# The diagonal of eight attention steps on TensorE, with values and state as separate factors

## The chip, the cores and the metric

The kernel runs on one core of a Trainium2 chip. The metric is the time of one execution on the device in microseconds, the median of several runs. A profiled execution has a time of its own, and a span from its first to its last instruction, on which every row of the trace is placed.

## What is computed

A linear attention with decay over 768 tokens (4 batches, 8 heads, head dimension 48), and behind it two dense two-layer blocks over the 3072 resulting tokens of width 384, inner width 2048. Weights arrive in double precision.

```python
for t in range(S):
    cur = np.einsum('bhd,bhe->bhde', u[None] * kt, vt)
    y[:, :, t] = np.einsum('bhd,bhde->bhe', rt, state + cur)
    state = wt[:, :, :, None] * state + np.einsum('bhd,bhe->bhde', kt, vt)
...
h = x @ w_in                    # block 1
g = np.where(h >= 1, h, np.where(h <= -1, 0.0, (h + 1) ** 2 / 4))
x = g @ w_out
...
h = x @ w_in                    # block 2
g = np.where(h > 0.0, h, np.exp(np.minimum(h, 0.0)) - 1.0)
out = g @ w_out
```

## The kernel before

**Attention.** The tokens are cut into chunks of 64; a step takes one chunk of all heads of two batches, so there are 24 steps of 128 tokens, each with the work of 16 heads in two halves of the 128 partitions (`hh`) and eight columns of tiles (`u`). Steps 0 to 3 make the first block of 512 tokens (`BLOCKS[0]`), and write it straight into the input tile `x_hl` of the dense block (`out_x`, `x_act`); the later ones go through the DRAM tensor `xd` (`out`, `out_act`). `QuotientAttention.stages` gives a step's seven stages: `decays` (two scans over the decays, L444 and L447, and one product in place that scales k and r, both in the tile `rk_sb`, L448), `operands` (a transpose of k on TensorE, copies of r into `tt` by `r_act`, L316 and L317, and the diagonal term: from k and r in token-major form, `tok_sb`, two products L458 and L460, a sum L462, and a spread of the sums onto the diagonal of `a_sb`, L464), `scores` (16 products of k and r on TensorE, L471; decay of the state, L356), `masked` (the state is copied into the free halves of the value tile `vs_sb`, L336 and L337; the scores under the mask are written into `a_sb`, L485), `placed` (`a_sb` is copied into the free halves of `tt`, L488 and L489; update of the state, L366 and L372), `out` (one product per tile: values stacked on the state, times scores stacked on r, L343 or L424) and `stored`. The stacking is what the four copies into `tt` and the two into `vs_sb` are for: 64 partitions hold values and scores, the other 64 state and r.

**Dense blocks.** Six parts of 512 tokens, each through two blocks, make 12 jobs (`ji`) of 16 slots (`f`). A slot multiplies into `h` (9 matmuls, L175), applies the activation (`act1` or `act2`, on ScalarE alone or on ScalarE and VectorE by `ON_ACT`), splits the result into a high and a low part (L220, L221) and multiplies into `y` (9 matmuls, L230). The weights of a slot are converted from double precision first (`weight_stages`, L121 to L139, five instructions on VectorE and three on ScalarE).

**Order.** Nothing loops at run time: everything is put into a plan by tick and rank (`at`), sorted, and emitted in that order; the framework then orders each engine's instructions by it and by what is ready in its own model. Step s begins at its tick in `START` (0, 4, 9, 12) or `AT1`, `AT2`, `AT`, relative to `t0` = 29 or to a job; its stages take one tick each with the ranks `RANK_A`. Weights of slot f begin at `WSTART[f]`, and the first slot runs at tick 29. So steps 0 to 7 lie ahead of the slots or beside the first two of them. `TOK_POOL` names the diagonal instructions that GpSimd takes instead of VectorE, `WARM` the numbers of matmuls on zeros that are issued in the first four steps' stages (L154), with no result that is used.

**Buffers.** `rk_sb` and `w_sb` have two buffers each, so step s+2 is loaded when step s no longer reads; `tok_sb` and `a_sb` have one, `vs_sb` and `tt` two. In PSUM `h` has two, the attention's transpose, scores and updates share two.

## Time and profile before

| | |
|---|---|
| runs, us | 942.51, 942.46, 940.45; median 942.46 |
| profiled execution, us | 942.46 |
| its span, us | 940.6 |
| TensorE busy (weight loads) | 97% (78%) |
| VectorE, ScalarE, GpSimd busy | 67%, 62%, 3% |
| mean granted TensorE clock | 0.98 of 2.4 GHz |

Shares over the whole span hide that the span has stages with different limits. It is read by stretches: for each, which engine is full, and whether TensorE, which is nearly always shown as busy, also loads weights at the rate that it has where nothing else is near its limit.

### The profile page before, as it was taken

How to read it: one execution, taken by the hardware profiler on the slowest of the kernel's cores; microseconds unless marked ns; L12 is line 12 of the kernel's file. 1: busy time of each engine (PE TensorE's matmuls, PEld its weight loads, DVE VectorE, ACT ScalarE, POOL GpSimd, SP SyncE). 2: the span in 40 equal slices, each digit the busy share in tenths (PEclk: the TensorE clock that was granted, in tenths of full speed). 3: DMA queues.
4: the chain of work that ended last, by engine and by line, in shares of the span. 5: the costliest groups of instructions: out<-in, count | busy, mean ns of one | idle time of the engine just before them, and what ended most of it. 6: DMA issues, size and time to landing. Idle time of an engine off the chain costs nothing. (4 is left out here: it accounts for less than half of the span.)

```text
span 940.6 us, 15005 instructions
## 1 busy us (share of the span) xinstructions
PE 911.7 (97%) x5985; PEld 736.7 (78%) x5985; DVE 634.1 (67%) x929; ACT 584.6 (62%) x944; POOL 29.0 (3%) x41
## 2 busy tenths in 40 slices
PE   9767999999999999999999999999999999999996
PEld 4555778788888888888888888888888888888885
DVE  8999999976566667643499995554554555555452
ACT  5778999886688877877799963433433423423332
POOL 1001001000010000000000000000000000000000
PEclk9958999999999999999999999999999999999998
DMA  7866644452234324321554400100200201000001
GB/s 222 272 213 212 234 151 145 140 166 60 93 94 127 110 87 125 111 84 25 178 200 135 167 35 1 49 20 1 67 1 1 68 1 32 35 1 1 34 1 37
DMA packets 42014, 87.81 MB, mean 93 GB/s; under 512 B 5072, under 2 KB 18512, under 8 KB 41936
## 3 DMA queue, kind: packets, MB, share of 16 engines
q1 hardware_dynamic: 41936, 86.77, 28.6%
q8 instruction: 49, 0.80, 0.4%
q14 instruction: 29, 0.24, 0.1%
HBM read 72.59 MB, written 14.16 MB: 92 GB/s over the span
## 5 line engine op out<-in xcount | busy, mean ns | idle before, releaser
L230 PE MATMUL y<-g_hl,w_hl 128*128 128x512 f32 x1728 | 429.7, 392 | 0.0
L175 PE MATMUL h<-x_hl,w_hl 128*128 128x512 f32 x1728 | 427.2, 391 | 1.7 <-ACT w_hl L138 0.8
L175 PEld LDWEIGHTS h<-x_hl,w_hl 128*128 128x128 f32 x1728 | 323.7, 188 | 71.1 <-DVE e_g L195 2.1
L230 PEld LDWEIGHTS y<-g_hl,w_hl 128*128 128x128 f32 x1728 | 321.1, 188 | 67.9 <-ACT g_hl L220 0.3
L221 DVE TENSOR_TENSOR g_hl<-e_g,g_hl 128x512 fp32r<-128x512 f32 x192 | 134.3, 700 | 102.4 <-ACT g_hl L220 102.0
L220 ACT CAST g_hl<-e_g 128x512 fp32r<-128x512 f32 x192 | 119.6, 623 | 101.7 <-DVE e_g L213 77.7
L210 ACT ACTIVATE e_g<-e_g 128x512 f32<-128x512 f32 x92 | 58.1, 632 | 153.1 <-DVE e_g L209 153.1
L213 DVE SCALAR_TENSOR_TENSOR e_g<-e_g,h 128x512 f32<-128x512 f32 x96 | 66.0, 687 | 60.8 <-ACT e_g L210 57.0
L209 DVE TENSOR_SCALAR e_g<-h 128x512 f32<-128x512 f32 x92 | 63.6, 691 | 44.0 <-PE h L175 43.4
L195 DVE TENSOR_TENSOR e_g<-h,e_g 128x512 f32<-128x512 f32 x96 | 65.7, 685 | 38.5 <-ACT e_g L188 38.3
L186 ACT ACTIVATE e_g<-h,half 128x512 f32<-128x512 f32 x87 | 60.2, 692 | 35.1 <-PE h L175 34.7
L187 ACT ACTIVATE e_g<-e_g,one 128x512 f32<-128x512 f32 x87 | 63.6, 731 | 1.5
L188 ACT ACTIVATE e_g<-e_g 128x512 f32<-128x512 f32 x87 | 55.6, 639 | 1.0
L366 PEld LDWEIGHTS ds<-vk_sb,rk_sb 64*64 64x64 f32 x704 | 20.8, 138 | 20.6 <-DVE st L372 7.7
L366 PE MATMUL ds<-vk_sb,rk_sb 64*64 64x48 f32 x704 | 24.4, 226 | 10.7 <-DVE st L372 6.6
L448 DVE TENSOR_TENSOR rk_sb<-rk_sb,w_sb 128x1024 f32<-128x1024 f32 x24 | 30.0, 1252 | 4.7 <-DMA rk_sb<-in_rkq 4.5
L471 PEld LDWEIGHTS sc<-tt,rk_sb 64*64 64x64 f32 x768 | 27.7, 144 | 6.9 <-issue 4.0
L139 DVE TENSOR_TENSOR w_hl<-w_z,w_hl 128x768 fp32r<-128x768 f32 x32 | 30.6, 958 | 3.1 <-ACT w_hl L138 3.0
L471 PE MATMUL sc<-tt,rk_sb 64*64 64x64 f32 x768 | 32.2, 233 | 0.2 <-ACT tt L488 0.2
L133 DVE CUSTOM_DVE_ANT_0 w_z<-w_raw,w_z 128x1536 uint16<-128x1536 uint16 x32 | 31.3, 977 | 0.5 <-ACT w_raw L122 0.2
L444 DVE TENSOR_TENSOR_SCAN w_sb<-w_sb,start 128x520 f32<-128x520 f32 x24 | 29.6, 1234 | 2.5 <-DMA w_sb<-in_wq 2.4
L464 POOL TENSOR_TENSOR a_sb<-eyef,z_sb 128x512 f32<-128x512 f32 x17 | 21.3, 1254 | 324.7 <-DMA xd<-a_sb 138.4
(65 smaller groups left out, 613.8 us busy)
## 6 DMA issues: line engine op xcount, KB each, us to landing
w_raw<-in_w SPq DMA_DIRECT2D x32, 768.0 KB, 4.7
rk_sb<-in_rkq SPq DMA_DIRECT2D x24, 512.0 KB, 3.9
tok_sb<-in_tokq SPq DMA_DIRECT2D x24, 384.0 KB, 3.3
w_sb<-in_wq SPq DMA_DIRECT2D x24, 260.5 KB, 3.9
x2d<-y_o SPq DMA_DIRECT2D x21, 256.0 KB, 2.0
x_hl<-x2d SPq DMA_DIRECT2D x6, 768.0 KB, 4.4
out_y<-y_o SPq DMA_DIRECT2D x18, 256.0 KB, 2.0
vk_sb<-in_vkq SPq DMA_DIRECT2D x22, 192.0 KB, 4.0
```

The source lines that it names most:

```text
L175: self.nc.tensor.matmul(h[:, :n], w[:, a, k * P:(k + 1) * P], x[:, b, k, :n], start=i == 0, stop=i == 8)
L186: nc.scalar.activation(out=g, in_=h[:, :n], func=AF.Relu, bias=self.half, scale=-0.5)
L187: nc.scalar.activation(out=g, in_=g, func=AF.Relu, bias=self.one, scale=-1.0)
L188: nc.scalar.activation(out=g, in_=g, func=AF.Square)
L195: nc.vector.tensor_tensor(out=g, in0=h[:, :n], in1=g, op=ALU.max)
L209: nc.vector.tensor_scalar_min(g, h[:, :n], 0.0)
L210: nc.scalar.activation(out=g, in_=g, func=AF.Exp)
L213: nc.vector.scalar_tensor_tensor(out=g, in0=g, scalar=1.0, in1=h[:, :n], op0=ALU.subtract, op1=ALU.max)
L220: nc.scalar.copy(gh[:, 0, :n], g)
L221: nc.vector.tensor_tensor(out=gh[:, 1, :n], in0=g, in1=gh[:, 0, :n].bitcast(F32), op=ALU.subtract)
L230: self.nc.tensor.matmul(y[d][:, :n], w[:, a, DM + d * P:DM + (d + 1) * P], g[:, b, :n], start=first and j == 0, stop=last and j == 2)
L471: nc.tensor.matmul(ps[64 * hh:64 * hh + 64, u], c["rk"][q:q + 64, 0, NU - 1 - u], c["tt"][q:q + 64, hh, u], start=True, stop=True)
```

## The change

For the steps below `DIAG` = 8:

- The diagonal term no longer comes from `tok_sb`. `diagonal`, at the head of `decays`, scales k by u per partition (four ScalarE instructions of 128x128 into `tt`), multiplies it with r on TensorE (16 products into a PSUM tile that shares the two buffers of `h`), and `operands` multiplies the result by the identity into `tt` (one VectorE instruction). The token loads, the two products, the sum and the spread are left out. A tile `u_col` with u along the partitions is loaded once by two DMAs.
- Values and state aren't stacked. The scores stay where they are masked (`c["a"]` is half of `tt`), r is read from `rk_sb`, the state is copied to a tile of zeros (`sz`), and `out` or `out_x` multiply twice into the same PSUM: values times scores, and state times r (the first step of a sequence once). The four copies into `tt` are left out. The halves of `vs_sb` that hold no values are set to zero on GpSimd.

The GpSimd share changes (`TOK_POOL`: the spread of steps 12 and later stays on GpSimd, that of steps 8 to 11 is on VectorE), one slot of job 0, two of job 1 go from ScalarE alone to both engines and job 6 has one more on ScalarE (`ON_ACT`), 24 matmuls on zeros fewer are issued, and ticks and ranks of the plan are others.

```diff
--- before.py
+++ after.py
@@ -31,26 +31,27 @@
 
 
 START = [0, 4, 9, 12]
-AT1 = [-13, -10, -7, -3]
-AT2 = [8, 13, 17, 20]
+AT1 = [-14, -11, -8, -4]
+AT2 = [7, 13, 17, 20]
 AT = [-6, 0, 3, 6]
 T0 = 11
-WSTART = [21, 22, 20, 25, 24, 29, 33, 37, 37, 39, 37, 42, 44, 44, 46, 46]
+WSTART = [21, 22, 21, 25, 27, 29, 33, 34, 37, 36, 37, 42, 43, 43, 45, 45]
 W2, W2_STEP = 4, 1.65
 X_POOL = [0, 1, 1] + [ji % 2 ^ 1 for ji in range(3, 12)]
 W_AHEAD, X_AHEAD, X_SPLIT = 1, 2, 1
 
-RANK_W = [[148, 62, -48], [103, 102, -10]]
-RANK_A = [[80, 146, 173, 72, 35, 21, 85], [39, 103, 199, 65, -3, 0, -18]]
-RANK_S = [[-38, 51, 56, -11, -26], [-4, 37, 46, 56, -7]]
-
-ON_ACT = {0: 27501, 5: 28415, 6: 34836}
-TOK_POOL = {(6, 1), (7, 1), (7, 2), (6, 0)} | {(s, 2) for s in range(8, NSTEP)}
+RANK_W = [[148, 66, -48], [97, 102, -10]]
+RANK_A = [[80, 109, 173, 72, 35, 21, 56], [25, 103, 199, 36, -3, 0, 53]]
+RANK_S = [[-38, 51, 71, -11, -26], [-4, 37, 46, 94, -7]]
+
+ON_ACT = {0: 27493, 1: 49119, 5: 28415, 6: 9268}
+DIAG = 8
+TOK_POOL = {(s, 2) for s in range(12, NSTEP)}
 RAW = {f: NF // 2 + f for f in range(NF // 2)} | {10: 14, 11: 15}
 SPLIT = 7
 NMORE = 5
 
-WARM = [[3, 3, 3, 3, 3, 3, 3], [1, 2, 0, 3, 2, 2, 2], [2, 1, 4, 3, 4, 1, 2], [3, 2, 2, 1, 2, 3, 2]]
+WARM = [[3, 3, 3, 3, 3, 3, 3], [1, 1, 0, 1, 1, 1, 1], [1, 1, 1, 1, 1, 1, 1], [1, 1, 1, 1, 1, 1, 1]]
 LIMIT = 2.0 ** 64
 
 
@@ -293,6 +294,10 @@
 
         return u
 
+    def apart(self, s):
+
+        return False
+
     def load_consts(self):
         self.nc.sync.dma_start(self.u_sb, self.io["ur"])
         self.nc.sync.dma_start(self.idt, self.io["ident"])
@@ -306,6 +311,9 @@
         s, nc = c["s"], self.nc
         t = self.a1.tile([P, 2, NU * CH], F32, name="vs_sb", bufs=2)
         c["vs"] = vs = t[:, :, :NU * vx.shape[-1]].rearrange("p h (u d) -> p h u d", u=NU)
+        if self.apart(s):
+            nc.gpsimd.memset(t[64:128, 0], 0.0)
+            nc.gpsimd.memset(t[0:64, 1], 0.0)
         nc.sync.dma_start(vs[0:64, 0], vx[s, 0])
         nc.sync.dma_start(vs[64:128, 1], vx[s, 1])
         if not c["last"]:
@@ -332,9 +340,9 @@
         self.nc.scalar.copy(c["kT"], c["ktp"])
 
     def state_act(self, c):
-        st = self.st
-        self.nc.scalar.copy(c["vs"][64:128, 0, :, :D], st[64:128].rearrange("p a b d -> p (a b) d"))
-        self.nc.scalar.copy(c["vs"][0:64, 1, :, -D:], st[0:64].rearrange("p a b d -> p (a b) d"))
+        st, to = self.st, c.get("sz", c["vs"])
+        self.nc.scalar.copy(to[64:128, 0, :, :D], st[64:128].rearrange("p a b d -> p (a b) d"))
+        self.nc.scalar.copy(to[0:64, 1, :, -D:], st[0:64].rearrange("p a b d -> p (a b) d"))
 
     def out(self, c):
         av, nc = self.av, self.nc
@@ -380,6 +388,7 @@
     def __init__(self, tc, ctx, io, xd):
         super().__init__(tc, ctx, io, xd, 2, 2)
         nc, c = self.nc, self.const
+        self.zs = {}
         self.eye = c.tile([P, 2, CH], I32, name="eye")
         self.eyef = c.tile([P, CH], F32, name="eyef")
         self.start = [c.tile([P, NU, CE], F32, name=f"start{i}") for i in range(2)]
@@ -391,6 +400,9 @@
     def vu(self, u):
         return NU - 1 - u
 
+    def apart(self, s):
+        return s < DIAG
+
     def kT_tile(self, c):
         return c["rk"][:, 0].rearrange("p (a b) c -> p a (b c)", b=2)
 
@@ -401,6 +413,10 @@
         super().load_consts()
         self.nc.sync.dma_start(self.eye, self.io["eyeq"])
         self.nc.sync.dma_start(self.eyef, self.io["eyefq"])
+        self.u_col = self.const.tile([P, 4, 1], F32, name="u_col")
+        self.nc.gpsimd.memset(self.u_col, 0.0)
+        for o, row in ((0, 64), (64, 0)):
+            self.nc.sync.dma_start(self.u_col[o:o + D], self.io["ur"][row:row + 1].rearrange("o p d -> d p o"))
 
     def load(self, s):
         c, nc, io = self.new(s), self.nc, self.io
@@ -409,20 +425,46 @@
         c["rk"] = self.a2.tile([P, 2, NU, CH], F32, name="rk_sb")
         nc.sync.dma_start(c["rk"], io["rkq"][s])
 
+    def sz(self, s):
+
+        n = CH if s < BLOCKS[0] else D
+        if n not in self.zs:
+            z = self.a1.tile([P, 2, NU, D], F32, name="tok_sb") if n == D else self.place()
+            self.nc.gpsimd.memset(z, 0.0)
+            self.zs[n] = z
+        return self.zs[n]
+
     def load_tok(self, c):
         c["tok"] = self.a1.tile([P, 2, NU, D], F32, name="tok_sb")
         self.nc.sync.dma_start(c["tok"], self.io["tokq"][c["s"]])
 
+    def factors(self, c, hh, u):
+
+        if c["s"] >= DIAG:
+            return [(c["vs"][:, hh, self.vu(u)], c["tt"][:, hh, u])]
+        return [(c["vs"][:, hh, self.vu(u)], c["a"][:, u])] + [(c["sz"][:, hh, self.vu(u)], c["rk"][:, 1, u])] * (not c["first"])
+
+    def out(self, c):
+        av, nc = self.av, self.nc
+        for u in range(NU):
+            for hh in range(2):
+                h = self.factors(c, hh, u)
+                for i, (v, t) in enumerate(h):
+                    nc.tensor.matmul(av[64 * hh:64 * hh + D, u], v, t, start=i == 0, stop=i == len(h) - 1)
+
     def out_x(self, c):
 
         nc = self.nc
         av = c["av"] = self.av.rearrange("p u c -> p (u c)")[:, :3 * TS].rearrange("p (k b t) -> p k b t", k=3, b=2)
         for b in range(2):
             for k, parts in ((0, ((0, 0),)), (1, ((1, 32),)), (2, ((0, 32), (1, 0)))):
-                for i, (hh, o) in enumerate(parts):
+                n = len(self.factors(c, 0, 0))
+                for i in range(n * len(parts)):
+                    hh, o = parts[i // n]
                     for p in range(4):
-                        nc.tensor.matmul(av[32 * p:32 * p + 32, k, b], c["vs"][:, hh, self.vu(2 * p + b), o:o + 32],
-                                         c["tt"][:, hh, 2 * p + b], start=i == 0, stop=i == len(parts) - 1)
+                        v, t = self.factors(c, hh, 2 * p + b)[i % n]
+                        nc.tensor.matmul(av[32 * p:32 * p + 32, k, b], v[:, o:o + 32], t,
+                                         start=i == 0, stop=i == n * len(parts) - 1)
 
     def x_act(self, c, x, t):
 
@@ -439,7 +481,21 @@
         def flat(t):
             return t.rearrange("p u c -> p (u c)")
 
+        def diagonal():
+            ku = c["tt"][:, 1]
+            for p in range(4):
+                j = NU - 2 - 2 * p
+                nc.scalar.activation(out=ku[:, j:j + 2], in_=c["rk"][:, 0, j:j + 2], func=AF.Copy, scale=self.u_col[:, p])
+            c["z"] = z = self.ph.tile([P, NU * CH], F32, name="z", tag="h").rearrange("p (u c) -> p u c", u=NU)
+            for u in range(NU):
+                for hh in range(2):
+                    q = 64 - 64 * hh
+                    nc.tensor.matmul(z[64 * hh:64 * hh + 64, u], ku[q:q + 64, NU - 1 - u], c["rk"][q:q + 64, 1, u],
+                                     start=True, stop=True)
+
         def decays():
+            if s < DIAG:
+                diagonal()
             back, w = c["w"][:, :NU * CE], c["w"][:, NU * CE:2 * NU * CE]
             nc.vector.tensor_tensor_scan(out=back, data0=free_ap(c["w"], 0, P, 2 * NU * CE, [[-1, NU * CE]]),
                                          data1=flat(self.start[0]), initial=0.0, op0=ALU.mult, op1=ALU.add)
@@ -450,9 +506,14 @@
         def operands():
             if not c["last"]:
                 self.k_transpose(c, c["rk"][:, 0])
-            self.r_act(c, c["rk"][:, 1])
+            if s >= DIAG:
+                self.r_act(c, c["rk"][:, 1])
             w = free_ap(c["w"], 0, P, 0, [[CE, 2 * NU], [1, CH]])
             nc.scalar.activation(out=w, in_=w, func=AF.Square, accum_out=self.sums[:, s:s + 1])
+            a = c["a"] = c["tt"][:, 0] if s < DIAG else self.a1.tile([P, NU, CH], F32, name="a_sb")
+            if s < DIAG:
+                nc.vector.tensor_mul(a, free_ap(self.eyef, 0, P, 0, [[0, NU], [1, CH]]), c["z"])
+                return
             tok = c["tok"]
             e = [nc.gpsimd if (s, i) in TOK_POOL else nc.vector for i in range(3)]
             e[0].tensor_mul(tok[:, 0].rearrange("p (a b) d -> p a b d", b=2), tok[:, 0].rearrange("p (a b) d -> p a b d", b=2),
@@ -460,7 +521,6 @@
             e[1].tensor_mul(tok[:, 0], tok[:, 0], tok[:, 1])
             z = self.a1.tile([P, NU], F32, name="z_sb")
             nc.vector.tensor_reduce(out=z, in_=tok[:, 0], op=ALU.add, axis=AX.X)
-            a = c["a"] = self.a1.tile([P, NU, CH], F32, name="a_sb")
             e[2].tensor_mul(a, free_ap(self.eyef, 0, P, 0, [[0, NU], [1, CH]]), free_ap(z, 0, P, 0, [[1, NU], [0, CH]]))
 
         def scores():
@@ -468,8 +528,8 @@
             for u in range(NU):
                 for hh in range(2):
                     q = 64 - 64 * hh
-                    nc.tensor.matmul(ps[64 * hh:64 * hh + 64, u], c["rk"][q:q + 64, 0, NU - 1 - u], c["tt"][q:q + 64, hh, u],
-                                     start=True, stop=True)
+                    nc.tensor.matmul(ps[64 * hh:64 * hh + 64, u], c["rk"][q:q + 64, 0, NU - 1 - u],
+                                     (c["rk"][:, 1] if s < DIAG else c["tt"][:, hh])[q:q + 64, u], start=True, stop=True)
             if not c["last"]:
                 self.k_act(c)
             if c["first"]:
@@ -478,15 +538,16 @@
                 self.decay_state(free_ap(c["w"], 0, P, CH, [[CE, NU], [0, D]]))
 
         def masked():
-            self.state_act(c)
-            if x is not None:
-                nc.gpsimd.memset(c["vs"][64:128, 0, :, D:], 0.0)
-                nc.gpsimd.memset(c["vs"][0:64, 1, :, :16], 0.0)
+            if s < DIAG:
+                c["sz"] = self.sz(s)
+            if not (c["first"] and s < DIAG):
+                self.state_act(c)
             nc.vector.copy_predicated(c["a"], free_ap(self.eye, 0, P, 0, [[0, NU], [1, CH]]), c["sc"])
 
         def placed():
-            nc.scalar.copy(c["tt"][0:64, 0], c["a"][0:64])
-            nc.scalar.copy(c["tt"][64:128, 1], c["a"][64:128])
+            if s >= DIAG:
+                nc.scalar.copy(c["tt"][0:64, 0], c["a"][0:64])
+                nc.scalar.copy(c["tt"][64:128, 1], c["a"][64:128])
             if not c["last"]:
                 self.state_pe(c)
                 self.state_add(c)
@@ -677,6 +738,8 @@
         moe = Moe(tc, mctx)
         actx = ExitStack()
         att = QuotientAttention(tc, actx, io, xd)
+        att.ph = moe.ph
+        att.place = lambda: moe.place(NF - 1)[0].tile([P, 2, NU, CH], F32, name="state_z", tag="w")
         moe.staging(actx, 2, 3)
         plan = {}
 
@@ -719,7 +782,8 @@
                 at(0, 0, lambda: ys.update({0: [moe.py[0].tile([P, 512], F32, name=f"y{d}") for d in range(3)]}))
                 at(0, 1, lambda: moe.warm(ys[0][0], 6))
             at(tick - 4 if tick >= 4 else 0, 0 if tick < 4 else 85, load)
-            at(max(tick - 1, 0), 86, lambda: att.load_tok(att.ctx[s]))
+            if s >= DIAG:
+                at(tick - 1, 86, lambda: att.load_tok(att.ctx[s]))
             at(tick + 1, 87, lambda: att.load_v(att.ctx[s], io["vxp" if s < BLOCKS[0] else "vxq"], io["vkq"]))
             for i, rank in enumerate(RANK_A[int(s >= BLOCKS[0])]):
                 at(tick + i, rank, lambda i=i: st["s"][i]())
```

## Rows read from the trace of the kernel before

**Rows 1.** Table of windows: stretch, length, busy us (instructions) by engine, clock, DMA share, GB/s.
```profile
25.00:40.00 15.00, 12.94 (x340) 8.95 (x339) 14.33 (x26) 10.45 (x19) 0.40 (x2) 1.00 0.83 259
40.00:64.00 24.00, 13.02 (x174) 10.83 (x171) 22.93 (x34) 16.91 (x28) 2.19 (x2) 0.58 0.69 235
64.00:85.00 21.00, 15.77 (x185) 12.16 (x184) 18.31 (x30) 15.49 (x24) 1.60 (x1) 0.75 0.70 235
95.00:130.00 35.00, 34.63 (x204) 27.57 (x204) 35.00 (x52) 34.12 (x56) 1.64 (x1) 1.00 0.62 205
130.00:170.00 40.00, 40.00 (x316) 32.31 (x314) 39.81 (x62) 39.38 (x65) 3.07 (x1) 1.00 0.47 150
200.00:300.00 100.00, 100.00 (x826) 81.40 (x826) 63.62 (x96) 74.46 (x123) 5.78 (x5) 1.00 0.35 108
```

**Rows 2.** Timeline, VectorE, 32 to 37 us: start, us, instruction, idle before it.
```profile
32.66 0.56 DVE L458 TENSOR_TENSOR tok_sb<-tok_sb,u_sb 128x384 f32<-128x384 f32 x1 [0.67 <-DMA tok_sb<-in_tokq]
...
34.07 1.23 DVE L444 TENSOR_TENSOR_SCAN w_sb<-w_sb,start 128x520 f32<-128x520 f32 x1
35.23 0.53 DVE L462 TENSOR_REDUCE z_sb<-tok_sb 128x8 f32<-128x384 f32 x1
35.67 0.20 DVE L446 RECIPROCAL start<-w_sb 128x8 f32<-128x8 f32 x1
35.85 0.69 DVE L464 TENSOR_TENSOR a_sb<-eyef,z_sb 128x512 f32<-128x512 f32 x1
36.46 0.55 DVE L432 TENSOR_TENSOR x_hl<-av,x_hl 128x384 fp32r<-128x384 f32 x1
```

**Rows 3.** Timeline, VectorE where GpSimd works too, steps 6 and 7.
```profile
58.13 2.01 DVE L448 TENSOR_TENSOR rk_sb<-rk_sb,w_sb 128x1024 f32<-128x1024 f32 x1
...
82.98 0.55 DVE L462 TENSOR_REDUCE z_sb<-tok_sb 128x8 f32<-128x384 f32 x1 [0.90 <-POOL tok_sb L460]
...
90.84 1.80 DVE L133 CUSTOM_DVE_ANT_0 w_z<-w_raw,w_z 128x1536 uint16<-128x1536 uint16 x1
```

**Rows 4.** Groups by form, whole span: count, busy us, mean ns, idle before.
```profile
L195 DVE TENSOR_TENSOR e_g<-h,e_g 128x512 f32<-128x512 f32 x96 | 65.7, 685 | 38.5 <-ACT e_g L188 38.3
L133 DVE CUSTOM_DVE_ANT_0 w_z<-w_raw,w_z 128x1536 uint16<-128x1536 uint16 x32 | 31.3, 977 | 0.5 <-ACT w_raw L122 0.2
L448 DVE TENSOR_TENSOR rk_sb<-rk_sb,w_sb 128x1024 f32<-128x1024 f32 x24 | 30.0, 1252 | 4.7 <-DMA rk_sb<-in_rkq 4.5
L349 ACT COPY a_sb<-av 128x512 f32<-128x512 f32 x20 | 11.4, 572 | 1.2 <-issue 1.2
L190 ACT ACTIVATE e_g<-h,half 128x512 f32<-128x512 f32 x9 | 6.4, 710 | 1.9 <-PE h L175 1.9
L431 ACT CAST x_hl<-av 128x384 fp32r<-128x384 f32 x4 | 1.9, 464 | 0.0
L388 POOL MEMSET start<- 128x520 f32 x2 | 1.0, 534 | 0.0
```

**Rows 5.** Timeline, TensorE: scores at either clock, matmuls on zeros.
```profile
18.43 1.15 PE L471 MATMUL sc<-tt,rk_sb 64*64 64x64 f32 x32
...
34.25 1.48 PE L154 MATMUL y<-zero 128*128 128x512 bf16 x6
...
41.52 2.19 PE L471 MATMUL sc<-tt,rk_sb 64*64 64x64 f32 x32
```

**Rows 6.** Timeline: L448 of steps 0 and 2, and the reload of rk.
```profile
6.38 1.23 DVE L448 TENSOR_TENSOR rk_sb<-rk_sb,w_sb 128x1024 f32<-128x1024 f32 x1
...
16.53 0.33 SPq L410 DMA_DIRECT2D rk_sb<-in_rkq  x1
...
20.61 1.21 DVE L448 TENSOR_TENSOR rk_sb<-rk_sb,w_sb 128x1024 f32<-128x1024 f32 x1
```

**Rows 7.** Timeline: a GpSimd memset with a VectorE product beside it.
```profile
18.63 0.20 POOL L484 MEMSET vs_sb<- 64x128 f32 x1
18.65 0.53 DVE L458 TENSOR_TENSOR tok_sb<-tok_sb,u_sb 128x384 f32<-128x384 f32 x1
```

## The prediction

> **What bounds the kernel now.** I read three views in this order. First the table of windows [rows 1]: busy time of each engine in stretches of the span. The reader is to see three regimes. From 25 to 85 us VectorE (DVE) is busy 14.33 + 22.93 + 18.31 = 55.6 of 60 us (93%), TensorE (PE) only 12.94 + 13.02 + 15.77 = 41.7 of 60, and its granted clock falls to 0.58 and 0.75 in the mean, so part of even that work ran at the lower level, 1.2 GHz. From 95 us on PE is full, and from 130 to 170 us PE, DVE and ScalarE (ACT) are all full. From 200 us on DVE is down to 64%, PE stays at 100%. Whether PE is at its own rate from 130 to 170, or only looks busy while it waits for DVE, is read from the weight loads: their share is 32.31/40 = 81%, as in 200:300 (81.40/100), where DVE cannot be the limit. So from about 100 us PE does its remaining list at full rate, and an edit pays only if it lets this regime begin earlier: what comes before is a start-up set by DVE. It holds the eight attention steps that the change touches and the first weight conversions.
>
> Second, the DVE timeline inside the start-up [rows 2]: the instructions stand shoulder to shoulder, each begins about 0.08 us before the one ahead of it has ended, so a removed instruction is worth the distance between starts, not its duration. Third, the places where DVE and GpSimd (POOL) run side by side [rows 3], and the typical durations [rows 4].
>
> The profiled execution took 942.46 us, which is also the median of the runs, for a span of 940.6: the sum below is made on the span, and the same 1.9 us lie around it afterwards.
>
> **DVE, what goes.** In each of steps 0 to 7 the diagonal's token-major work goes: two products, a sum and a spread onto the diagonal. By distance between starts the product is taken at 0.48 (its duration 0.56 less the overlap), the sum 35.67 - 35.23 = 0.44, the spread 36.46 - 35.85 = 0.61 [rows 2]: 2 x 0.48 + 0.44 + 0.61 = 2.01. One instruction comes in its place: identity times the scores that PE left in PSUM, the same 128x512, taken at the 0.61 of the spread, since DVE's product L195 of the same shape with an operand from PSUM lasts 685 ns [rows 4], as long as the spread's 0.69 [rows 2]. Net 1.40 per step, for steps 0 to 5 8.4. Step 6 has its two products on POOL: there the sum and the spread (1.05) go, the new product (0.61) comes, and the 128x1024 product beside POOL took 2.01 instead of 1.25 [rows 3, 4], 0.76 more. That is 1.2. Step 7 has one product on DVE (0.48), an idle 0.90 in front of the sum while POOL finishes, the sum (0.44), and a weight instruction that took 1.80 beside POOL's spread against 0.98 [rows 3, 4], less 0.61: 2.0. The idle 0.67 for the landing of the token tile [rows 2] goes with its load. Together 8.4 + 1.2 + 2.0 + 0.7 = 12.3 us of a DVE-bound stretch.
>
> The Trainium skill, "SBUF — State Buffer", section on the doors into SBUF, says that VectorE and GpSimd share a port pair that is locked for a whole instruction, so that the other one "fully blocks". The two stretched rows agree in kind. By that rule alone step 6 would give back POOL's whole two products rather than 0.76, about 1.4 us more in the sum. The same rule speaks against the change's new POOL memsets, 16 of 64x512, against DVE instructions in a two-port mode. The rows show a memset beside a DVE product with two inputs that took its ordinary 0.53 [rows 7], and none beside the other kind: memsets are charged nothing; if each of the eight in steps 4 to 7 blocked DVE for its length (0.53 at 128x520 [rows 4]), that would be 4.2 us.
>
> **DVE, what comes back.** (a) The start. The first 128x1024 product of rk began at 6.38 us [rows 6], as soon as its operands were there. Now a column of u must land first (two more DMAs of single elements in the queue of SP, issued behind the constants and in front of step 1's loads, at 0.33 us an issue or more [rows 6]), then ACT scales k (1.2, below) and PE does 32 diagonal passes (1.15 [rows 5]). If the column lands with rk, that is 2.35 us later than 6.38; the scans of step 1 can fill a part. Bounds 0.5 and 4 us, taken at 2.0. (b) In every step the product L448 overwrites rk in place, so it must now wait for the diagonal, which reads rk before it. ACT's part: four 128x128 with a scale from memory; from 710 ns at 512 columns and (572 - 464)/128 = 0.84 ns a column [rows 4], 710 - 384 x 0.84 = 387 ns each, some 1.2 us overlapped. PE's part: 1.15 at full clock, 2.19 at the lower one, as the scores' 32 [rows 5]. Chain about 2.5 to 3.7 us with hand-overs; the two scans and the reciprocal in front of L448 cover about 2.4 (35.23 - 34.07 = 1.16 for a scan, twice, and a little for the reciprocal [rows 2]). Behind a stalled L448 everything on DVE waits, weight conversion too. Bounds 0 and 2.3 us a step; taken at 0.3 for seven steps, 2.0, since a step's operands usually lie there long before its scans. (c) Behind 95 us DVE gets four spreads back from POOL (steps 8 to 11) and three activations move partly from ACT (one slot of job 0, two of job 1): 7 x 0.6 = 4.2 us in a stretch where DVE is 99% busy [rows 1]; fewer stretched instructions and the emptier DVE from 170 on take most of it. Bounds 0 and 4.2, taken at 1.0.
>
> Sum: 12.3 - 2.0 - 2.0 - 1.0 = 7.3 us.
>
> **The other engines.** ACT loses four copies of 512 columns a step (some 0.57 each, by the 128x512 one [rows 4]) and gains 4 x 0.39: 0.7 us less a step. It was less busy than DVE from 25 to 85 [rows 1], so I count this at nothing; the way from the masked scores to the output gets two copies, 1.1 us, shorter. The eight token loads of 384 KB leave SP's queue and the DMA engines (share 0.83 from 25 to 40 us [rows 1]): a cover, not a term. PE gains 32 passes of diagonal a step (1.15), a second set of passes for the output of steps 1 to 7 (taken as the scores' too, 1.15) and loses 24 warm-up matmuls (1.48/6 = 0.25 each, 6 us, mostly ahead of 25 us) [rows 5]. Of that some 6 x 1.15 + 7 x 1.15 = 15.0 us, less about ten warm-ups, 2.4, fall between 25 and 85, 12.6 us into an idle of 18.3. This leaves 5.7 us by which the stretch can shrink before PE binds, if the clock stays as it was; were it at 2.4 GHz throughout, 13.02 x 0.42 + 15.77 x 0.25 = 9.4 us more. So PE allows a gain between 5.7 and 15.1, and the 7.3 lies inside it, near the lower end.
>
> **Who holds rk.** Before, rk's buffer is free after the state update: its reload for step 2 was issued at 16.53, and L448 of step 2 began at 20.61 [rows 6], practically at the landing. Now the output reads r straight out of rk, so the reload comes after the output, by 1.15 us and a hand-over or more later, and the diagonal stands between landing and L448. In steps 2 to 4 this chain (reload 4.1, diagonal 2.5, product 1.25, scores 1.15, then mask, state and an output of 2.3: some 12 to 13 us for two steps) is about as long as two steps of DVE's own work. I count on it being hidden there, since outputs come earlier as well.
>
> **Rivals.** (1) The gain is eaten in the start: the rk chain holds steps 1 to 5 at their old distance, so that their 5 x 1.4 = 7 us are idle time instead, or PE binds at the low clock. Then 0 to 2 us are left: about 941. For it: L448 of step 2 had no slack; against: DVE was 96% busy from 25 to 40 us, so it seldom stood waiting for a reload there. (2) Slower: the diagonal is not hidden behind the scans. With PE at the lower clock and ACT one pair of copies behind, the chain is 3.7 + 1.0, less 2.4 of cover, so L448 stalls 2.3 us in each of eight steps, 18.4, against 12.3 - 3.0 of net savings: 9 us slower, about 951. It decides from (12.3 - 3.0)/8 = 1.2 us of stall per step. For it: the clock is low from 40 to 64 us, and fewer warm-ups remain. Against: the loads are issued steps ahead, so the diagonal can run before DVE comes to the scans. (3) Better: no stall, and the fuller PE keeps its clock: 12 to 15 us, 928 to 930.
>
> **How the numbers follow.** Forecast 942.46 - 7.3 = 935. Chances: forecast with its bounds (930 to 939.5) 0.58, rival 3 0.12, rival 1 0.16, rival 2 0.14. About 0.3% (2.8 us) is what a measurement of this kernel can tell from no change: faster 0.70, same 0.16, slower 0.14. The range leaves out rival 2's far part and the tip of rival 3: 926 to 945.
>
> **What would show it.** Right: the groups L458, L460 and L462 count 16 instead of 24 each; DVE busy from 10 us to the point where the share of weight loads reaches 80% is shorter by some 9 us; that point lies some 7 us earlier; the stretch behind it is of unchanged length. Wrong: idle time in front of L448 released by PE or ACT above 1.2 us a step (rival 2); reloads of rk later than before with DVE idle behind them, or PE busy over 95% already from 40 us (rival 1). The prediction as a whole would fail if the regime behind 100 us was not PE's: then the moved DVE work would show there as new PE gaps.

## The result, and the profile after

The changed kernel took 933.04 us (median of four runs, 931.84 to 936.03), the kernel before 942.42 (four runs, 940.45 to 942.51): a ratio of 0.991, 95% interval 0.989 to 0.9925. That is 9.4 us less. Forecast were 935.0, in a range of 926 to 945. The profiled execution of the changed kernel took 931.84 for a span of 930.0, against 942.46 and 940.6 before, so 10.6 us have to be found in the two traces.

First the table of windows of the changed kernel, in the stretches and columns of [rows 1] (busy time of TensorE, of its weight loads, of VectorE, ScalarE and GpSimd; then clock, DMA share, GB/s):

```profile
25.00:40.00 15.00, 10.46 (x325) 8.72 (x316) 15.00 (x24) 11.13 (x22) 2.08 (x4) 1.00 0.77 252
40.00:64.00 24.00, 19.63 (x540) 17.46 (x540) 23.49 (x37) 19.29 (x39) 3.12 (x6) 0.93 0.70 228
64.00:85.00 21.00, 19.15 (x307) 15.82 (x304) 20.62 (x33) 17.10 (x31) 0.00 (x0) 1.00 0.70 208
95.00:130.00 35.00, 34.93 (x235) 27.83 (x234) 34.77 (x53) 33.93 (x57) 0.00 (x0) 1.00 0.37 119
130.00:170.00 40.00, 40.00 (x300) 32.32 (x298) 39.79 (x61) 35.15 (x59) 0.00 (x0) 1.00 0.40 127
200.00:300.00 100.00, 100.00 (x842) 81.00 (x842) 64.14 (x98) 74.29 (x121) 4.29 (x4) 1.00 0.35 105
```

From 25 to 85 us VectorE (DVE) is busy 15.00 + 23.49 + 20.62 = 59.1 of 60 us, before 55.6 [rows 1]: the start-up is still DVE's, more so than before. TensorE (PE) does 49.2 us of work there instead of 41.7, and its granted clock is 0.93 and 1.00 where it was 0.58 and 0.75. From 130 us on the rate of the weight loads has not changed: they take 32.32 of 40 us, before 32.31 [rows 1]. So the gain lies ahead of that. How much lies there can be counted. These are the matmuls of the dense blocks, called expert matmuls below (the lines L175 and L230, one row each) in the window up to 100 us of the kernel before: busy us and count on PE, then clock, DMA share, GB/s:

```profile
0.00:100.00 100.00, 14.59 (x49) 0.85 0.71 231
0.00:100.00 100.00, 4.85 (x18) 0.85 0.71 231
```

And of the changed kernel (L176 and L231):

```profile
0.00:100.00 100.00, 16.19 (x64) 0.98 0.75 238
0.00:100.00 100.00, 10.85 (x45) 0.98 0.75 238
```

That is 67 before and 109 after, 42 more. What one is worth shows late in the changed kernel, in a window where PE does nothing else:

```profile
800.00:900.00 100.00, 100.00 (x443) 82.84 (x442) 51.10 (x74) 31.73 (x52) 0.00 (x0) 1.00 0.02 9
```

443 in 100 us are 0.226 us each, and 42 x 0.226 = 9.5 us: nine tenths of the 10.6 are won by 100 us. (Both traces hold all 3456 expert matmuls, 12 jobs of 16 slots with 18 each, so the counts lack none.)

What DVE did to get there is read from its groups up to 100 us. Before:

```profile
L448 DVE TENSOR_TENSOR rk_sb<-rk_sb,w_sb 128x1024 f32<-128x1024 f32 x8 | 10.5, 1316 | 0.1
L133 DVE CUSTOM_DVE_ANT_0 w_z<-w_raw,w_z 128x1536 uint16<-128x1536 uint16 x7 | 7.5, 1070 | 0.0
L139 DVE TENSOR_TENSOR w_hl<-w_z,w_hl 128x768 fp32r<-128x768 f32 x6 | 5.7, 949 | 2.4 <-ACT w_hl L138 2.4
L464 DVE TENSOR_TENSOR a_sb<-eyef,z_sb 128x512 f32<-128x512 f32 x7 | 4.8, 684 | 0.0
L462 DVE TENSOR_REDUCE z_sb<-tok_sb 128x8 f32<-128x384 f32 x8 | 4.3, 541 | 0.9 <-POOL tok_sb L460 0.9
L458 DVE TENSOR_TENSOR tok_sb<-tok_sb,u_sb 128x384 f32<-128x384 f32 x7 | 3.9, 552 | 0.9 <-DMA tok_sb<-in_tokq 0.9
L460 DVE TENSOR_TENSOR tok_sb<-tok_sb 128x384 f32<-128x384 f32 x6 | 3.3, 552 | 0.1
```

After (the lines have moved: L448 is now L504, L133 is L134, L139 is L140, and L515 is the new product):

```profile
L504 DVE TENSOR_TENSOR rk_sb<-rk_sb,w_sb 128x1024 f32<-128x1024 f32 x9 | 10.9, 1215 | 0.5 <-PE z L493 0.4
L134 DVE CUSTOM_DVE_ANT_0 w_z<-w_raw,w_z 128x1536 uint16<-128x1536 uint16 x8 | 7.6, 951 | 0.0
L140 DVE TENSOR_TENSOR w_hl<-w_z,w_hl 128x768 fp32r<-128x768 f32 x8 | 7.6, 956 | 0.0
L515 DVE TENSOR_TENSOR tt<-eyef,z 128x512 f32<-128x512 f32 x8 | 5.5, 683 | 0.0
```

Four groups of 16.3 us in all are gone and 5.5 us came for them; the groups that had instructions beside GpSimd (POOL) have their ordinary mean back (1316 to 1215, 1070 to 951 ns); the waits for the token tile and for POOL (0.9 each) are gone, and so is one that the prediction did not have, 2.4 us in front of the weights' last product, for ScalarE (ACT). The first finished slot, an input of the second matmuls, is the product L221, now L222. It began 12.4 us earlier. DVE's timeline before:

```profile
90.24 0.68 DVE L221 TENSOR_TENSOR g_hl<-e_g,g_hl 128x512 fp32r<-128x512 f32 x1
```

And after:

```profile
77.83 0.69 DVE L222 TENSOR_TENSOR g_hl<-e_g,g_hl 128x512 fp32r<-128x512 f32 x1
```

### The profile page after: what moved, and what is told of

Its sections match the earlier page's. It is cut to its first block, busy times and chain, and to the rows that moved or that the text cites. A ratio compares the mean times of both kernels' runs of the same rounds, so it can differ in the third digit from the quotient of the medians.

```text
span 930.0 us, 16053 instructions
## 1 busy us (share of the span) xinstructions
PE 908.0 (98%) x6533; PEld 741.8 (80%) x6537; DVE 622.3 (67%) x915; ACT 573.6 (62%) x937; POOL 25.9 (3%) x44
## 5 line engine op out<-in xcount | busy, mean ns | idle before, releaser
L231 PE MATMUL y<-g_hl,w_hl 128*128 128x512 f32 x1728 | 429.7, 393 | 0.1
L176 PE MATMUL h<-x_hl,w_hl 128*128 128x512 f32 x1728 | 424.4, 390 | 0.0
L176 PEld LDWEIGHTS h<-x_hl,w_hl 128*128 128x128 f32 x1728 | 323.5, 188 | 68.2 <-DVE e_g L196 0.3
L231 PEld LDWEIGHTS y<-g_hl,w_hl 128*128 128x128 f32 x1728 | 320.8, 188 | 68.1 <-ACT g_hl L221 0.8
L222 DVE TENSOR_TENSOR g_hl<-e_g,g_hl 128x512 fp32r<-128x512 f32 x192 | 133.2, 694 | 102.3 <-ACT g_hl L221 101.9
L221 ACT CAST g_hl<-e_g 128x512 fp32r<-128x512 f32 x192 | 118.7, 618 | 104.2 <-DVE e_g L214 77.1
L211 ACT ACTIVATE e_g<-e_g 128x512 f32<-128x512 f32 x91 | 57.5, 632 | 152.0 <-DVE e_g L210 152.0
L187 ACT ACTIVATE e_g<-h,half 128x512 f32<-128x512 f32 x84 | 57.4, 684 | 32.5 <-PE h L176 32.0
L188 ACT ACTIVATE e_g<-e_g,one 128x512 f32<-128x512 f32 x84 | 60.7, 722 | 1.6
L189 ACT ACTIVATE e_g<-e_g 128x512 f32<-128x512 f32 x84 | 53.0, 631 | 1.2
L504 DVE TENSOR_TENSOR rk_sb<-rk_sb,w_sb 128x1024 f32<-128x1024 f32 x24 | 29.3, 1219 | 6.5 <-DMA rk_sb<-in_rkq 6.0
L500 DVE TENSOR_TENSOR_SCAN w_sb<-w_sb,start 128x520 f32<-128x520 f32 x24 | 29.7, 1237 | 4.3 <-POOL st L536 2.2
L123 ACT ACTIVATE w_raw<-w_raw 128x768 int32<-128x768 uint32 x32 | 28.9, 908 | 3.9 <-DMA w_raw<-in_w 3.9
L140 DVE TENSOR_TENSOR w_hl<-w_z,w_hl 128x768 fp32r<-128x768 f32 x32 | 30.4, 954 | 1.1 <-ACT w_hl L139 0.9
L134 DVE CUSTOM_DVE_ANT_0 w_z<-w_raw,w_z 128x1536 uint16<-128x1536 uint16 x32 | 30.5, 952 | 0.5 <-ACT w_raw L123 0.2
L132 DVE SCALAR_TENSOR_TENSOR w_z<-w_raw,w_z 128x768 int32<-128x768 int32 x32 | 30.4, 950 | 0.2
L139 ACT CAST w_hl<-w_z 128x768 fp32r<-128x768 f32 x32 | 26.5, 830 | 5.7 <-DVE w_z L134 5.7
L503 DVE TENSOR_TENSOR_SCAN w_sb<-w_sb,start 128x520 f32<-128x520 f32 x24 | 29.7, 1239 | 0.5
L512 ACT ACTIVATE w_sb<-w_sb 128x1024 f32<-128x1024 f32 x24 | 25.4, 1056 | 7.0 <-DVE rk_sb L504 6.8
```

Source lines behind the costliest of these rows:

```text
L134: nc.vector.tensor_tensor(out=zi, in0=zi, in1=c["raw"][:, :, 0], op=ALU.add)
L176: self.nc.tensor.matmul(h[:, :n], w[:, a, k * P:(k + 1) * P], x[:, b, k, :n], start=i == 0, stop=i == 8)
L187: nc.scalar.activation(out=g, in_=h[:, :n], func=AF.Relu, bias=self.half, scale=-0.5)
L188: nc.scalar.activation(out=g, in_=g, func=AF.Relu, bias=self.one, scale=-1.0)
L189: nc.scalar.activation(out=g, in_=g, func=AF.Square)
L211: nc.scalar.activation(out=g, in_=g, func=AF.Exp)
```

## The experiments

The theory, A, is that of the prediction: the start-up is DVE's, the gain is the work taken from DVE, so the diagonal on PE carries it, and the copies that fall away on ACT are worth little. Its first rival, P: the plan (start times, ranks and warm-ups, which the change rewrites too) does it, and the mechanism little. Further letters in the expectations name rival accounts of the run at hand. "The old plan" below means the constants of the kernel before, "the new plan" those of the changed kernel. The medians of the kernel before in these runs were 941.8 to 941.9.

### The plan without the mechanism, and the mechanism without the plan

The kernel before, with the new constants:

```
-AT1 = [-13, -10, -7, -3]
-AT2 = [8, 13, 17, 20]
+AT1 = [-14, -11, -8, -4]
+AT2 = [7, 13, 17, 20]
...
-RANK_A = [[80, 146, 173, 72, 35, 21, 85], [39, 103, 199, 65, -3, 0, -18]]
+RANK_A = [[80, 109, 173, 72, 35, 21, 56], [25, 103, 199, 36, -3, 0, 53]]
...
-ON_ACT = {0: 27501, 5: 28415, 6: 34836}
+ON_ACT = {0: 27493, 1: 49119, 5: 28415, 6: 9268}
```

> The kernel before, with the ticks, ranks, weight starts, warm-up numbers and ScalarE shares of the changed kernel, and its GpSimd share for steps 8 to 11; diagonal and stacking as before. Theory A (the gain is VectorE's work taken out of the start-up): 942, at most 2 us faster. Rival P (the gain is the plan's, above all the weights begun earlier): 933 to 936.

Measured: 949.3 us, ratio 1.0078 (1.0049 to 1.0106). Neither theory had that: the new plan alone costs 7.4 us. The changed kernel, with the old constants (the same lines the other way round):

> The changed kernel with the ticks, ranks, weight starts, warm-ups and shares of the kernel before. Theory A: 933 to 937, most of the gain stays. Rival P: 940 or more.

Measured: 938.6, ratio 0.9965 (0.9948 to 0.9981). The mechanism alone gains 3.3 us, and the plan is worth 5.6 more on top of it. P falls, since the plan without the mechanism loses; but A as I first had it, with all of the gain from the mechanism, falls as well. The plan fits the work that it was made for and no other.

### Half of the mechanism

The diagonal on PE, everything else as before (r copied to two places, diagonal scores copied beside it, values and state stacked). A second constant splits the two halves of the change, first in the new plan:

```
-DIAG = 8
+DIAG, APART = 8, 0
...
-        if c["s"] >= DIAG:
+        if c["s"] >= APART:
             return [(c["vs"][:, hh, self.vu(u)], c["tt"][:, hh, u])]
...
-            if s >= DIAG:
+            if s >= APART:
                 self.r_act(c, c["rk"][:, 1])
```

> The changed kernel with the diagonal on TensorE, but values and state stacked by copies again (four ScalarE copies a step more, half the passes of the output, no second factor). Theory A: 933 to 937, since the copies lie on ScalarE, which is not the bound of the start-up, and the VectorE instructions are gone. Rival S (the copies on the way from scores to output are what cost): 939 to 943.

Measured: 950.58, ratio 1.0102 (1.0081 to 1.0124). And with the old plan:

> The kernel before with the diagonal on TensorE alone, stacking, ticks, ranks and shares as before. Theory A: 935 to 938. Theory B (the scaling of k fills ScalarE unless the copies go, so each part alone is worth little): 941 to 946, as the same half showed in the new plan.

Measured: 950.27, ratio 1.0086 (1.0066 to 1.0106). All that was expected was too low, A's figures by more than 12 us: the diagonal alone takes the product sums off DVE, and the kernel is 8.4 us slower than before. A fell here, and so did the account of the second run that calls each part alone worth little (B, 941 to 946). The other half, products kept apart with the diagonal still from token-major tiles (0 and 8 in the line above; the zeroed state tile of steps 4 to 7 lies elsewhere, since the token tiles are still in use), new plan and old plan:

> The changed kernel with values and state apart, but the diagonal from the token-major products again, in steps 6 and 7 on GpSimd as before. Theory A: 940 to 944, the 12 us of VectorE are back. Rival S: 933 to 937.

> The kernel before with values and state apart alone, the diagonal from the token-major products, ticks, ranks and shares as before. Theory A: 941 to 943. Theory B: 939 to 942, some gain from the four copies, the rest only with the diagonal.

Measured: 945.2, ratio 1.005 (1.003 to 1.007), and 943.69, ratio 1.0021 (1.0005 to 1.0037). Both lie above all that was expected of them; for the second, B had some gain. So, by plan:

| medians, us | neither half | diagonal | apart | both | both, less what the halves add up to |
|---|---|---|---|---|---|
| old plan | 941.9 | 950.3 (+8.4) | 943.7 (+1.8) | 938.6 (-3.3) | -13.5 |
| new plan | 949.3 | 950.6 (+1.3) | 945.2 (-4.1) | 933.0 (-16.3) | -13.5 |

Neither half beats the kernel before in either plan, and together they gain. The last column is the same in both plans. (Each cell has an instruction order of its own, which is worth some 5 us by itself, below, and the last column adds up four of them, so the 13.5 is no exact figure.) By these runs, then, the halves need each other. B's reason for it, that the copies that fall away on ACT make the room for the diagonal's scaling, is looked for in the stretch from 12 to 85 us, in the columns of [rows 1]. The kernel before:

```profile
12.00:85.00 73.00, 54.49 (x890) 39.51 (x889) 67.99 (x109) 51.37 (x86) 4.58 (x7) 0.79 0.72 234
```

Diagonal alone, old plan:

```profile
12.00:85.00 73.00, 57.89 (x1146) 44.35 (x1148) 65.39 (x101) 66.15 (x124) 0.80 (x4) 0.86 0.70 232
```

Apart alone, old plan:

```profile
12.00:85.00 73.00, 57.58 (x1195) 44.80 (x1197) 70.62 (x112) 38.48 (x64) 11.24 (x17) 0.88 0.76 244
```

The changed kernel:

```profile
12.00:85.00 73.00, 60.44 (x1505) 50.84 (x1504) 71.07 (x111) 57.05 (x105) 6.24 (x12) 0.98 0.74 237
```

The diagonal alone takes ACT from 51.37 to 66.15 us of 73 (91%; from 40 to 64 us it is busy 23.67 of 24, and DVE 23.69), and DVE falls to 65.39: it has less to do and does it no sooner. Apart alone empties ACT to 38.48 and leaves DVE its whole list (70.62). Only both together leave DVE shorter work (71.07, all of it further on in the list) and ACT room (57.05). Which engine waits for which is read from ACT's groups in that stretch. Before:

```profile
L316 ACT COPY tt<-rk_sb 64x512 f32<-64x512 f32 x7 | 4.3, 616 | 10.1 <-DVE rk_sb L448 10.0
L488 ACT COPY tt<-a_sb 64x512 f32<-64x512 f32 x7 | 4.3, 616 | 6.1 <-DVE a_sb L485 6.1
```

Diagonal alone, old plan (L324 is the old L316, L552 the old L488, and L488 now the scaling of k):

```profile
L488 ACT ACTIVATE tt<-rk_sb,u_col 128x128 f32<-128x128 f32 x26 | 8.7, 393 | 0.1
L324 ACT COPY tt<-rk_sb 64x512 f32<-64x512 f32 x7 | 4.3, 618 | 1.2 <-DVE rk_sb L504 1.1
L552 ACT COPY tt<-a_sb 64x512 f32<-64x512 f32 x7 | 4.3, 617 | 0.2 <-DVE a_sb L548 0.2
```

Before, ACT stood 16.2 us waiting for DVE in front of these copies; that is what made it look free. With the diagonal alone it waits 1.4 us: the 8.7 us of scaling and 5.5 more of weight conversion in this stretch have filled it. PE's longest wait there is now for the scaling:

```profile
PE z L493 <- ACT tt L488: 3.4, 3, 3.0
```

On DVE the same trace shows a wait for the state's products where the kernel before had 0.5 us:

```profile
L380 DVE TENSOR_TENSOR st<-st,ds 128x192 f32<-128x192 f32 x16 | 5.2, 348 | 5.6 <-PE ds L374 5.6
```

That ACT is what makes the pair is argued from these waits, not shown by a run that changes ACT's load alone with the order held. What held up the state's products isn't traced to ACT (PE's own waits in front of them are for a DMA, 2.4 us, and for DVE, 1.7). And by 100 us this kernel is 44 expert matmuls far, the kernel before 67: 5.2 of its 8.4 us, of which some were lost from 85 to 100 us, where neither ACT (12.40 of 15 us) nor DVE (13.09) is full.

### Is the start-up DVE's? Work added on one engine

Work added on one engine in each of the first eight steps of the changed kernel. In each of the three an instruction group that is there already is issued again (twice more on DVE, once more on ACT and PE), with the same result. DVE, identity times the scores three times:

```
             if s < DIAG:
-                nc.vector.tensor_mul(a, free_ap(self.eyef, 0, P, 0, [[0, NU], [1, CH]]), c["z"])
+                for _ in range(3):
+                    nc.vector.tensor_mul(a, free_ap(self.eyef, 0, P, 0, [[0, NU], [1, CH]]), c["z"])
```

> The changed kernel with the product of identity and diagonal scores made three times in steps 0 to 7: 2 x 0.61 x 8 = 9.8 us more on VectorE. If VectorE's sum sets the start-up (theory A): 941 to 943. If the start-up now waits for something else (theory B: the start is balanced between VectorE, ScalarE and the order of loads): 933 to 938.

Measured: 949.48, ratio 1.0079 (1.0062 to 1.0096): 16.4 us above the changed kernel, for 16 x 0.61 = 9.8 us of added DVE time; both figures expected were too low. ACT, the scaling of k twice:

```
-            for p in range(4):
+            for p in (0, 1, 2, 3) * 2:
```

> The changed kernel with k scaled by u twice in steps 0 to 7: four ScalarE instructions more a step, some 1.2 us each step, 9.6 in all, and as much in front of the in-place product. Theory A (ScalarE has room, as the prediction counted): 933 to 935. Theory B (ScalarE is nearly the bound too, and only the removed copies pay for the scaling; this would explain why the diagonal alone brought nothing): 938 to 943.

Measured: 942.01, ratio 1.0009 (0.9999 to 1.0018): 9.0 us more, for some 9.6 added. PE, the diagonal's matmuls twice:

```
-            for u in range(NU):
+            for u in [*range(NU)] * 2:
```

> The changed kernel with the diagonal products made twice in steps 0 to 7: 32 passes more a step, 1.15 us, 9.2 in all on TensorE, and as much in front of the in-place product. If TensorE has room in the start-up and the wait is hidden: 933 to 935, perhaps less, as the clock is held better. If it binds: 940 or more.

Measured: 945.31, ratio 1.0032 (1.002 to 1.0045): 12.3 more, for some 9.2 added. DVE's price is the highest, as A wanted; but ACT and PE, which A had at little, cost about their whole addition or more, and DVE's costs more than it adds. Not all of it lies in the start-up. By 100 us the three kernels are 62, 73 and 55 expert matmuls far, the changed one 109: 10.6, 8.1 and 12.2 us behind, so that the start-up alone doesn't set DVE's price above PE's. What DVE's costs beyond that comes later, above all from 130 to 150 us, where PE waits; here first that kernel, then the changed one:

```profile
130.00:150.00 20.00, 16.48 (x101) 13.15 (x98) 15.98 (x25) 16.45 (x28) 0.00 (x0) 0.83 0.20 63
130.00:150.00 20.00, 20.00 (x145) 16.25 (x144) 20.00 (x31) 17.04 (x28) 0.00 (x0) 1.00 0.39 125
```

In all three the planner also ordered the other instructions differently, so these are prices of work and of order together. Two runs take them apart.

### The order held: work beside DVE

Two GpSimd products in each of the first eight steps, of which nothing is read. The order of the instructions on DVE, PE, ACT and the load queue is that of the changed kernel, so only what GpSimd does to DVE is left, and what its own memsets are delayed by:

```
                 nc.vector.tensor_mul(a, free_ap(self.eyef, 0, P, 0, [[0, NU], [1, CH]]), c["z"])
+                for _ in range(2):
+                    nc.gpsimd.tensor_mul(self.side, free_ap(self.eyef, 0, P, 0, [[0, 7], [1, CH]]), free_ap(self.eyef, 0, P, 0, [[1, 7], [0, CH]]))
```

> The changed kernel with two products of 128x448 on GpSimd in each of steps 0 to 7, whose result nobody reads. The order of instructions on TensorE, VectorE, ScalarE and the DMA queue is left exactly as it is; only VectorE is held up beside them (by 0.25 to 0.85 us each, as the rows of the kernel before showed). If VectorE sets the start-up: 16 such delays, 4 to 10 us, so 937 to 943. If not: 933 to 935.

Measured: 939.44, ratio 0.9973 (0.9961 to 0.9986), so 6.4 us above the changed kernel. DVE's groups from 12 to 85 us in this kernel (its L501 and L505 are L500 and L504 of the changed one):

```profile
L505 DVE TENSOR_TENSOR rk_sb<-rk_sb,w_sb 128x1024 f32<-128x1024 f32 x8 | 10.4, 1294 | 1.2 <-ACT w_raw L123 1.1
L501 DVE TENSOR_TENSOR_SCAN w_sb<-w_sb,start 128x520 f32<-128x520 f32 x6 | 8.4, 1393 | 0.2 <-DMA w_sb<-in_wq 0.2
L134 DVE CUSTOM_DVE_ANT_0 w_z<-w_raw,w_z 128x1536 uint16<-128x1536 uint16 x6 | 6.4, 1071 | 0.0
L132 DVE SCALAR_TENSOR_TENSOR w_z<-w_raw,w_z 128x768 int32<-128x768 int32 x6 | 6.3, 1052 | 0.0
L129 DVE TENSOR_SCALAR w_z<-w_z 128x768 f32<-128x768 f32 x7 | 5.4, 778 | 0.0
L364 DVE TENSOR_TENSOR st<-st,w_sb 128x384 f32<-128x384 f32 x7 | 4.6, 651 | 0.0
```

The same groups of the changed kernel:

```profile
L504 DVE TENSOR_TENSOR rk_sb<-rk_sb,w_sb 128x1024 f32<-128x1024 f32 x8 | 9.7, 1214 | 0.5 <-PE z L493 0.4
L500 DVE TENSOR_TENSOR_SCAN w_sb<-w_sb,start 128x520 f32<-128x520 f32 x6 | 7.4, 1240 | 0.0
L134 DVE CUSTOM_DVE_ANT_0 w_z<-w_raw,w_z 128x1536 uint16<-128x1536 uint16 x7 | 6.7, 951 | 0.0
L132 DVE SCALAR_TENSOR_TENSOR w_z<-w_raw,w_z 128x768 int32<-128x768 int32 x7 | 6.6, 939 | 0.0
L129 DVE TENSOR_SCALAR w_z<-w_z 128x768 f32<-128x768 f32 x8 | 4.4, 556 | 0.0
L364 DVE TENSOR_TENSOR st<-st,w_sb 128x384 f32<-128x384 f32 x7 | 3.9, 555 | 0.0
```

Mean against mean, times the count, DVE lost 8 x 0.08 + 6 x 0.15 + 6 x 0.12 + 6 x 0.11 + 7 x 0.22 + 7 x 0.10 = 5.2 us, and its idle time in front of L505 and L501 grew by 0.9. Since the order is the same, each DVE instruction can also be set beside its counterpart: up to 85 us they took 5.7 us more in all, the idle time before them grew by 0.1 in sum, and the delay, 6.2 us at the product that began at 32.88 us in the changed kernel, is still 6.3 at 130 us. The first finished slot came at 84.14 instead of 77.83 us, 6.3 later, and the end 5.9 later by the spans (935.9 and 930.0). What DVE loses in the start-up arrives at the end nearly whole: this is the run that shows the start-up to be DVE's. (In this trace the granted clock from 25 to 40 us was 0.61 instead of 1.00; PE was busy only 11.52 of 15 us there, so it had room, and with DVE's idle time 0.1 more in sum no cost of the lower clock can be seen.)

### The order alone

Two ranks of the planner changed, no work: about 60 of DVE's instructions change places.

```
-RANK_A = [[80, 109, 173, 72, 35, 21, 56], [25, 103, 199, 36, -3, 0, 53]]
+RANK_A = [[80, 146, 173, 72, 35, 21, 85], [25, 103, 199, 36, -3, 0, 53]]
```

> The changed kernel with the ranks of steps 0 to 3 as in the kernel before (two numbers, 109 to 146 and 56 to 85). No work is added or taken away; some 60 of VectorE's 2370 instructions change their place. If order alone moves the time by several microseconds, which would explain why an earlier start made the kernel slower: off 933 by 3 us or more, either way. If not: 932 to 935.

Measured: 938.26, ratio 0.9962 (0.9946 to 0.9977), 5.2 us above the changed kernel. Its stretch from 12 to 85 us:

```profile
12.00:85.00 73.00, 59.24 (x1524) 50.04 (x1529) 68.04 (x106) 53.21 (x99) 6.22 (x12) 0.95 0.71 227
```

DVE is idle 73 - 68.04 = 5.0 us there, in the changed kernel 1.9: 3.0 of the 5.2 us show as waiting on the engine that is the bound. With the plan's 5.6 us on the whole mechanism this makes the order a term of its own, of the size of the gains in question; and of the excess of the three kernels with added work, some 5 us each way cannot be put down to the work.

### The late start

In the changed kernel the first product L504 began at 11.47 us, before at 6.38 [rows 6]. ACT's timeline tells why:

```profile
6.76 1.28 ACT L488 ACT_TABLE_LOAD   x1 [6.76 <-DMA u_col<-in_ur]
8.05 1.28 ACT L488 ACTIVATE tt<-rk_sb,u_col 128x128 f32<-128x128 f32 x4
```

The scaling of k is ACT's first instruction, and the table load in front of it waits for the column of u as well. So I loaded the column later in the queue, right behind step 0's two loads, and gave ACT a copy at the head that takes the table load:

```
-        self.u_col = self.const.tile([P, 4, 1], F32, name="u_col")
...
+        if s == 0:
+            self.u_col = self.const.tile([P, 4, 1], F32, name="u_col")
+            nc.gpsimd.memset(self.u_col, 0.0)
+            nc.scalar.copy(self.sums[:, 0:1], self.start[0][:, 0, 0:1])
```

> The changed kernel with the column of u loaded right behind step 0's decays and k, r, in front of the constants, and with a ScalarE copy at the head, so that the activation table is there before the column lands. The first in-place product comes at some 8 us instead of 11.5. If the late start is carried through the start-up: 930 to 931. If it is made up by other work that VectorE had waiting: 933.

The first product began at 9.22, 2.3 us earlier, though not at the 8 expected. Measured: 937.87, ratio 0.9952 (0.9938 to 0.9967), which is 4.8 us slower than the changed kernel; neither figure expected had that. From 12 to 85 us DVE is idle 7.2 us instead of 1.9:

```profile
12.00:85.00 73.00, 60.10 (x1437) 50.24 (x1438) 65.77 (x102) 50.36 (x96) 6.46 (x12) 0.88 0.70 224
```

The order had changed here too, on DVE, ACT and the load queue, and more was lost behind the start than it gave. What 2.3 us of earlier start are worth in an unchanged order stays open. No kernel of these twelve beat the changed one.

## Why the prediction was right, and where not

**The bound.** Right. The start-up is DVE's (work beside DVE, order held, arrives at the end), PE's regime behind it is unchanged, and the gain is what was won by 100 us.

**What DVE saves**, 12.3 us forecast. From the two lists above: 16.3 - 5.5 = 10.8 us of busy time; L448, L133 and L129 back at their length, 8 x 0.10 + 7 x 0.12 + 7 x 0.12 = 2.5 (the last, now L130, from 657 to 538 ns); two waits of 0.9; less the overlap of 0.08 [rows 2] for the 20 instructions fewer, 1.6. Together 13.5: 1.2 more than forecast, within what the method can do. Of it 0.7 is a second instruction stretched beside GpSimd in step 6, a weight instruction of 1.30 us at 56.91 that the forecast had not counted.

**The start (a)**, 2.0 forecast, bounds 0.5 and 4. The first product came 5.1 us later, where I had written 2.35 before any filling: I had left out that the table load is not hidden any more, and that the column's two transfers stand 0.92 us in the load queue. But the product's start was the wrong clock to read. What counts is DVE's busy time up to 12 us, in a window of the kernel before:

```profile
0.00:12.00 12.00, 10.67 (x64) 4.78 (x65) 8.38 (x10) 5.20 (x9) 2.67 (x16) 1.00 0.81 243
```

And of the changed kernel:

```profile
0.00:12.00 12.00, 10.93 (x93) 5.36 (x95) 6.39 (x8) 3.84 (x9) 5.57 (x19) 1.00 0.80 234
```

8.38 - 6.39 = 2.0 us of work lost, the forecast value, in part by luck, because the scans of step 1 did come forward (9.85 us, ahead of the product at 11.47). Right sum, with one wrong size inside it and a cover larger than thought.

**The stall behind the diagonal (b)**, 2.0 forecast, measured 0.4 in step 0 (the line of L504 above), and 0.1 in all from step 1 on. The step's own argument, that operands lie there long before the scans, was right, and the value too high. Rival 2 needed 1.2 us a step; it fell.

**The work given back (c)**, 1.0 forecast. From 95 to 170 us the weight loads keep their rate (27.83 and 32.32, before 27.57 and 32.31 [rows 1]), so no cost of it can be seen.

**ACT, counted at nothing.** This is the step that failed: a gain that hangs on ACT's copies was charged to DVE alone. It did not move the sum's sign. I took ACT for free since it was less busy than DVE; the waits in front of its copies say that it was busy less because it waited for DVE, 16.2 us of its 21.6 idle. Without the copies removed, the diagonal makes the kernel 8.4 us slower, not 7 faster. And DVE gains the 2.4 us in front of L139 that it had stood waiting for ACT, a term that the sum did not have; whether it is owed to the copies is open, since with the diagonal alone, copies and all, that wait is gone too. A sum by engines has to ask of each engine that receives work how much of its idle time is left once the bound engine runs faster.

**The sum.** By 100 us: 13.5 + 2.4, less 2.0 (start), 0.4 (diagonal), 1.0 (more waiting for the state's products, 1.8 after against 0.8) gives 12.5, and the first finished slot was 12.4 earlier. Of this 9.5 were left at 100 us and 10.6 at the end. The loss is PE's: when the first slot was finished, the kernel before had started 31 expert matmuls (PE had run ahead while the slot waited for DVE), the changed one 18, and 13 x 0.226 = 2.9 us are what 12.4 and 9.5 differ by. Forecast were 7.3; the 12.5 are 1.2 more in DVE's list, 2.4 in ACT's wait, 1.6 in (b) and 1.0 in (c), less the 1.0 for the state's products.

**What the sum had no term for** is the plan. It is worth 5.6 us with this mechanism, by the runs, and -7.4 without it. With the old plan, 938.6, the 935.0 would have been 3.6 us too low. That the number is right is therefore in part luck: a term that was left out made up for it.

**The rivals.** Rival 1: rk's reload for step 2 was issued at 17.06 instead of 16.53 us [rows 6], and no DVE idle time stands behind it; PE was busy 60.44 of 73 us, not full. It fell, and the low clock that would have fed it did not come. Rival 3: its two conditions, no stall and a kept clock (0.93 from 40 to 64 us, before 0.58 [rows 1]), were met nearly whole, and still the time was 933 and not 928 to 930. What a kept clock is worth while DVE is the bound, no run here isolates.

**The marks set for it.** L519, L521 and L523 (the old L458, L460 and L462) count 16 instead of 24, as said. The share of weight loads was a poor mark: before, in stretches of ten us, it stands at 75% to 82% from 80 us to 200 and crosses 80% several times, so that "the point where it reaches 80%" is not sharp. The count of expert matmuls says the same thing better.

## What to carry to other kernels

Moving work from the bound engine to another helps, as these traces are read, only as far as the engine that receives it still has idle time once the bound one runs faster: read what its idle time waits for, and free it in the same change. Halves of such a change can each lose what both together gain, so that trying them singly says little of the pair. Where a planner orders the work, an experiment that lets it reorder measures work and order together; hold the order, or know its price (here 5 us, 0.5%).
